# Scaling and transposing the score matrix of an attention kernel: products with a diagonal, or a scale on VectorE and transposes on TensorE

## The chip, the cores and the metric

The kernel runs on one core of a Trainium2 chip. The metric is the time of one execution on the device, in microseconds (us); lower is better. The core has five engines that run side by side and wait for each other through semaphores: TensorE for matrix products (PE in the profile, with its loading of the stationary operand shown apart as PEld), VectorE (DVE), ScalarE (ACT), GpSimd (POOL) and SyncE (SP), which here only issues transfers. Data lie in device memory, in SBUF (128 partitions) or in PSUM, into which TensorE writes.

## The reference

Two steps follow each other. The first is an attention between channels: q, k and v have the shape 4 x 6208 x 256, q and k are normalised along the 6208 rows, and a 256 x 256 matrix of scores per batch goes through a softmax.

```python
def _attn_ref(q, k, v, tau):
    qn = q / (np.linalg.norm(q, axis=1, keepdims=True) + 1e-06)
    kn = k / (np.linalg.norm(k, axis=1, keepdims=True) + 1e-06)
    s = kn.transpose(0, 2, 1) @ qn / tau
    s = s - s.max(-1, keepdims=True)
    a = np.exp(s)
    a /= a.sum(-1, keepdims=True) + 1e-09
    return (v @ a).astype(np.float32)

def _moe_ref(x, mu_k, mu_r, w_k, w_v, w_r):
    x_prev = np.concatenate([np.zeros((B, 1, D), dtype=np.float32), x[:, :-1, :]], axis=1)
    xk = mu_k * x + (1.0 - mu_k) * x_prev
    xr = mu_r * x + (1.0 - mu_r) * x_prev
    k = np.maximum(xk @ w_k, 0.0)
    v = k * k @ w_v
    r = 1.0 / (1.0 + np.exp(-(xr @ w_r)))
    return (r * v).astype(np.float32)
```

The second step takes the first one's result as x; its inner width is 1024. tau is 1.0.

## The kernel before

The rows of q and k of one batch are read in groups of up to 512 rows. For each 128 rows TensorE adds a product of q and k (two matmuls of 128 x 256, line 182) to the raw scores S in PSUM, which hold q's channels in the partitions and k's channels in the free dimension, without any norm. The sums of squares for the norms are collected beside it. The raw S is thus q's channels by k's channels, while the softmax runs over q's channels for each of k's channels. So S has to be divided by q's norms, which lie along its partitions, and turned, so that k's channels come to lie in the partitions.

The function `softmax_pieces` holds this work as pieces, to be called one at a time:

- `evac` (line 265): ScalarE copies S from PSUM to the fp32 tile `s_sb`, two halves of 128 partitions x 256.
- `roots`, `pow2`: the four columns of norms, 256 of q and 256 of k, come into the tile `rn` (128 x 4).
- `invert` (lines 257 to 260): VectorE adds a small number, takes the reciprocal, and multiplies the fp32 identity `ident_f` (128 x 128) by each of the two columns of q's reciprocal norms. The result is `rq_d`, two diagonal matrices.
- `turn` (lines 269 to 273): four fp32 products on TensorE, each with a 128 x 128 block of `s_sb` as the stationary operand and one of the diagonals as the moving one. Each writes a block of the turned and scaled S into `st_ps` in PSUM.
- `exp` (line 280): two exponentials on ScalarE from `st_ps` into `e_sb`, with k's reciprocal norms `rk` as a scale per partition, and row sums in `sm`. No maximum is subtracted, since tau bounds the scores.
- `shares`, `weigh`, `weigh_dve`: the rows are divided by their sums and give the bf16 matrix `a_sb`.

Batch 0 is summed first, in a phase of its own in which the transfers of q and k come in from SyncE's queue. At its end the pieces are called at once, with filler products between them (`keep_warm`, line 513, whose results nobody reads) and with the transposes of v's first blocks (`v_transpose_pe`, line 331). `x_first` (line 365) then makes the first block of x from `a_sb`.

After that one loop runs over 48 blocks of 512 rows of x (12 per batch) and one block of the rows left over. Each block has eight slots, j = 0 to 7. In the slots TensorE does the block's products: x from v and `a_sb` (line 352), the wide product (`up`, line 423, into `kT_ps`), the narrow products (`down`, lines 456 and 460, into `vr_ps`), and in some slots the scores of the next batch (`unit`). ScalarE takes `kT_ps` out (line 428), takes x out (line 354), squares q and k for the norms (lines 163 and 165) and makes the gate (line 469). VectorE mixes x with its previous row (line 408), squares (line 441), multiplies by the gate (line 470) and adds the squares up (line 169). When a batch's scores are complete, its pieces go into a list, in which an empty entry passes a slot; one entry is taken per slot:

```python
        return [evac, fold, None, None, norms, roots, pow2, None, invert, None, None, turn, exp, shares, None, weigh]
```

The program order on each engine is the order in which the loop writes the instructions; there is no scheduler that moves them. Plain loads with a change of type go through GpSimd's queue, v's transposing transfers and the stores through SyncE's.

Of the kernel before, what the change touches and what calls it, by code (L numbers as in the profile page):

```python
# [10 lines left out]
F32 = mybir.dt.float32  # L11
# [7 lines left out]
def kernel(  # L19
# [13 lines left out]
    nc = tc.nc  # L33
    B, N, C = q.shape
    D = C
    DF = moe_w_k.shape[1]
    P = 128
# [12 lines left out]
    pn = ctx.enter_context(tc.tile_pool(name="pn", bufs=2))  # L50
# [6 lines left out]
    ident_f = const.tile([P, P], F32, name="ident_f")  # L57
# [30 lines left out]
    st_ps = {}  # L88
# [124 lines left out]
    def softmax_pieces(b):  # L213

        s_ps, ssq_ps = cov.pop(b) if b else cov[b]
        rn = pn.tile([P, 4], F32, name="rn")
        rq_d = pn.tile([P, C], F32, name="rq_d")
        s_sb = pn.tile([P, 2, C], F32, name="s_sb")
        e_sb = pn.tile([P, 2, C], F32, name="e_sb", bufs=1)
        mx = pn.tile([P, 2], F32, name="mx")  # L220
        sm = pn.tile([P, 2], F32, name="sm")
        rk = rn[:, 2:4]
        def copies():
            cov["ssq"] = pn.tile([P, 2 * C], F32, name="ssq", tag="ssq", bufs=1)
            nc.vector.tensor_copy(cov["ssq"], ssq_ps)

        def gather():

            cov["s"] = cov[b][0]
            bank[b] = ps.tile([P, 2 * C], F32, name="bank", tag="xT_ps", bufs=2)  # L230
            for i in range(4):
                nc.tensor.matmul(bank[b][:, C + i:C + i + 1], cov["ssq"][:, i * P:(i + 1) * P], thirty2[:, 0:1],
                                 start=i == 0, stop=False, skip_group_check=True)

        def fold():
            t = pq.tile([P, 2 * C], BF16, name="sq", tag="sq", bufs=1)
            nc.vector.tensor_tensor(t, sums[b][:, 0], sums[b][:, 1], op=OP.add)
            sums[b] = t

        def norms():  # L240
            bank[b] = ps.tile([P, 2 * C], F32, name="bank", tag="xT_ps", bufs=2)
            for t, rows in ((sums.pop((b, "left"))[:, 0], L), (sums.pop(b), P)):
                for i in range(4):
                    nc.tensor.matmul(bank[b][:, C + i:C + i + 1], t[:rows, i * P:(i + 1) * P], ones[:rows, 0:1],
                                     start=rows == L and i == 0, stop=rows == P, skip_group_check=True)

        def roots():
            if b == 0:
                nc.scalar.activation(rn, bank[b][:, C:C + 4], AF.Sqrt)
            else:  # L250
                nc.scalar.copy(rn, bank[b][:, C:C + 4])

        def pow2():
            nc.gpsimd.tensor_tensor(rn, rn, half, op=OP.pow)

        def invert():
            nc.vector.tensor_scalar_add(rn, rn, 1e-6)
            nc.vector.reciprocal(rn, rn)
            for h in range(2):
                nc.vector.tensor_scalar_mul(rq_d[:, h * P:(h + 1) * P], ident_f, rn[:, h:h + 1])  # L260
            if inv_tau != 1.0:
                nc.vector.tensor_scalar_mul(rk, rk, inv_tau)

        def evac():
            nc.scalar.copy(s_sb, s_ps)

        def turn():

            st_ps[b] = ps.tile([P, 2, C], F32, name="st_ps", tag="xT_ps", bufs=2)
            for ih in range(2):  # L270
                for dh in range(2):
                    nc.tensor.matmul(st_ps[b][:, ih, dh * P:(dh + 1) * P], s_sb[:, dh, ih * P:(ih + 1) * P],  # L272
                                     rq_d[:, dh * P:(dh + 1) * P], start=True, stop=True)

        def exp():
            for ih in range(2):
                if not bounded:
                    nc.vector.tensor_reduce(mx[:, ih:ih + 1], st_ps[b][:, ih], axis=AX, op=OP.max, negate=True)
                    nc.vector.tensor_tensor(mx[:, ih:ih + 1], mx[:, ih:ih + 1], rk[:, ih:ih + 1], op=OP.mult)
                nc.scalar.activation(e_sb[:, ih], st_ps[b][:, ih], AF.Exp, scale=rk[:, ih:ih + 1],  # L280
                                     bias=0.0 if bounded else mx[:, ih:ih + 1],
                                     accum_out=sm[:, ih:ih + 1])

        def shares():
            nc.gpsimd.tensor_tensor(sm, sm, minus[:, 0:2], op=OP.pow)

        def weigh():
            for ih in range(2):
                nc.scalar.activation(a_sb[:, b, ih, :], e_sb[:, ih], AF.Copy, scale=sm[:, ih:ih + 1])

        def weigh_dve():
            for ih in range(2):
                nc.vector.reciprocal(sm[:, ih:ih + 1], sm[:, ih:ih + 1])
                nc.vector.tensor_scalar_mul(a_sb[:, b, ih, :], e_sb[:, ih], sm[:, ih:ih + 1])

        if b == 0:
            return [copies, gather, roots, evac, invert, turn, exp, weigh_dve]

        return [evac, fold, None, None, norms, roots, pow2, None, invert, None, None, turn, exp, shares, None, weigh]


# [216 lines left out]
    for g in order(0):  # L518
        group_load(0, g)
        group_cast(0, g)  # L520
        if g == DIRECT + 1:
            copies, gather, roots, evac, invert, turn, exp, weigh = softmax_pieces(0)
            copies()
            gather()
        for s in range(sizes(0)[g]):
            unit_matmul(0, g, s)
        if 5 <= g <= DIRECT:
            keep_warm(3)
        if g == NB - 1:

            nc.gpsimd.tensor_copy(gate, groups[0, g][0][:, 0, 0, 0:1])
            v_load(0)
# [25 lines left out]
    def unit(ahead=2):  # L558

        if pos["mm"] >= len(units):  # L560
            return
        u = units[pos["mm"]]
        loads_upto()
        feed(max(ahead, 1))
        unit_matmul(*u)
        pos["mm"] += 1
        feed(ahead)
        if u[1:] == (NB, S - 1):
            chain.extend(softmax_pieces(u[0]))
            holds[0] = u[0]  # L570
# [144 lines left out]
```

## Time and profile before

| | us |
|---|---|
| median of 5 runs | 515.55 |
| the five runs | 515.28, 515.55, 515.14, 518.67, 518.8 |
| the profiled execution | 515.59 |
| its span | 513.8 |
| PE busy in the span | 495.2 (96%) |
| ACT busy | 450.6 (88%) |
| DVE busy | 439.9 (86%) |
| POOL busy | 99.3 (19%) |
| PE, the four turns (line 272), 32 matmuls | 4.3 |
| DVE, the eight multiplications of line 260 | 2.1 |

The span is the time from the first to the last instruction that the profiler shows; the execution's own time is 1.8 us longer. Busy time of PE counts matmuls from start to end, and these overlap, so neighbouring matmuls can begin at less than one's duration from each other: the distance from start to start (the pitch) is what one costs in a row of them. The granted clock is the share of its full clock that TensorE was given.

### The profile page before, as it was taken

What the parts mean: (1) busy time and instruction counts of PE and PEld (TensorE: products, weight loads), DVE (VectorE), ACT (ScalarE), POOL (GpSimd) and SP (SyncE); (2) the same over time, 40 slices, a digit from 0 to 9 for tenths busy, and PEclk for the clock granted to TensorE, in tenths of its full rate; (3) what the DMA queues carried; (4) which work ended last, traced back from release to release, by engine and by line L of the source; (5) the groups of instructions that cost most, each with busy time, mean ns of one, the idle gap of its engine ahead of it and who ended that gap; (6) DMA issues with size and microseconds to landing.
All of it is one profiled execution on the core that took longest, in us unless ns stands there. A gap on an engine that the chain in (4) does not pass through costs nothing.

```text
span 513.8 us, 9496 instructions
## 1 busy us (share of the span) xinstructions
PE 495.2 (96%) x3540; PEld 336.8 (66%) x3540; DVE 439.9 (86%) x725; ACT 450.6 (88%) x924; POOL 99.3 (19%) x146
## 2 busy tenths in 40 slices
PE   4979999989999999999999999999999999999996
PEld 2455666767576767666676667667666666666675
DVE  4556899999999999999989999999878787878884
ACT  6876999999899999999899999999887888878784
POOL 0044341223045123131233223000131100000000
PEclk9989999999999999999999999999999999999999
DMA  8999999999999999998499999925497783423123
GB/s 310 409 310 189 199 152 186 150 163 197 219 176 171 204 209 167 162 171 162 89 163 184 186 184 181 192 65 124 83 168 144 109 139 84 105 76 89 42 83 103
DMA packets 133462, 83.46 MB, mean 162 GB/s; under 512 B 50660, under 2 KB 126760, under 8 KB 133416
## 3 DMA queue, kind: packets, MB, share of 16 engines
q0 software_dynamic: 56592, 33.01, 49.6%
q1 hardware_dynamic: 76656, 49.72, 42.5%
q8 instruction: 27, 0.44, 0.4%
q10 hardware_dynamic: 168, 0.13, 0.1%
q14 instruction: 19, 0.16, 0.1%
HBM read 78.71 MB, written 25.43 MB: 203 GB/s over the span
## 4 chain that ended last, share of the span: by engine, by line
PE 78%; DMA 10%; DVE 6%; ACT 4%; issue 1%; SPq 0%; DVEq 0%
PE vr_ps L460 29%; PE kT_ps L423 28%; PE vr_ps L456 7%; PE xT_ps L352 7%; PE s_ps L182 5%; DMA f<-in_k_dram 5%; DMA vT<-v_bf 5%; DVE acc L169 1%; DVE xk L408 1%; ACT kr L428 1%; DVE kk L441 1%; ACT sq L163 1%; PE st_ps L272 1%; ACT xT L354 1%; DVE delta L398 1%
## 5 line engine op out<-in xcount | busy, mean ns | idle before, releaser
L428 ACT ACTIVATE kr<-kT_ps 128x512 bf16<-128x512 f32 (+1 forms) x392 | 232.6, 605 | 28.8 <-PE kT_ps L423 24.8
L423 PE MATMUL kT_ps<-xk,w_k_sb 128*128 128x512 bf16 (+1 forms) x784 | 231.2, 377 | 0.4 <-DVE xk L408 0.2
L460 PE MATMUL vr_ps<-w_v_sb,kk 128*128 128x256 bf16 x1536 | 230.8, 273 | 0.1
L460 PEld LDWEIGHTS <-kk 128*128 128x128 bf16 x1536 | 149.7, 98 | 58.6 <-DVE kk L441 0.8
L470 DVE SCALAR_TENSOR_TENSOR res<-res,vr_ps 128x256 f32<-128x256 f32 x192 | 80.0, 417 | 45.2 <-ACT res L469 45.0
L441 DVE TENSOR_TENSOR kk<-kr 128x1536 bf16<-128x1536 bf16 (+2 forms) x148 | 117.0, 791 | 0.2 <-ACT kr L428 0.2
L423 PEld LDWEIGHTS <-w_k_sb 128*128 128x128 bf16 x784 | 75.8, 98 | 28.6 <-issue 1.2
L169 DVE TENSOR_TENSOR acc<-acc,sq 128x1024 f32<-128x1024 f32 x69 | 84.1, 1219 | 0.0
L182 PE MATMUL s_ps<-qk 128*128 128x256 bf16 x392 | 73.7, 289 | 5.0 <-DVE qk L142 5.0
L469 ACT ACTIVATE res<-vr_ps 128x256 f32<-128x256 f32 x192 | 76.2, 397 | 1.3 <-PE vr_ps L460 1.3
L456 PE MATMUL vr_ps<-w_r_sb,xr 128*128 128x256 bf16 x384 | 73.3, 272 | 1.1 <-DVE res L470 1.1
L408 DVE SCALAR_TENSOR_TENSOR xk<-delta,mu_t,xT 128x512 bf16<-128x512 bf16 x96 | 71.4, 746 | 0.0
L408 DVE SCALAR_TENSOR_TENSOR xr<-delta,mu_t,xT 128x512 bf16<-128x512 bf16 x96 | 71.4, 746 | 0.0
L456 PEld LDWEIGHTS <-xr 128*128 128x128 bf16 x384 | 37.5, 98 | 46.3 <-issue 2.4
L354 ACT CAST xT<-xT_ps 128x512 bf16<-128x512 f32 x94 | 55.4, 589 | 13.0 <-PE xT_ps L352 12.9
L352 PE MATMUL xT_ps<-vT,a_sb 128*128 128x512 bf16 x188 | 55.9, 379 | 1.6 <-DMA vT<-v_bf 1.4
L136 POOL DMA_DIRECT2D qk<-in_q_dram x39 | 26.1, 669 | 144.2 <-ACT kr L428 65.6
L165 ACT ACTIVATE sq<-qk 128x1024 f32<-128x1024 bf16 (+1 forms) x49 | 50.8, 1037 | 0.0
L182 PEld LDWEIGHTS <-qk 128*128 128x128 bf16 x392 | 39.3, 102 | 16.8 <-issue 6.8
L315 POOL DMA_DIRECT2D v_bf<-in_v_dram x48 | 37.0, 773 | 50.3 <-DMA vT<-v_bf 21.5
L398 DVE TENSOR_TENSOR delta<-xT 128x1024 bf16<-128x1024 bf16 x48 | 32.9, 686 | 1.9 <-ACT xT L354 1.8
L144 ACT ACTIVATE qk<-f 128x1024 bf16<-128x1024 f32 (+2 forms) x28 | 26.1, 948 | 8.1 <-DMA f<-in_q_dram 5.2
(82 smaller groups left out, 214.2 us busy)
## 6 DMA issues: line engine op xcount, KB each, us to landing
out_dram<-res SPq DMA_DIRECT2D x47, 512.0 KB, 4.8
v_bf<-in_v_dram POOLq DMA_DIRECT2D x48, 256.0 KB, 9.6
qk<-in_q_dram POOLq DMA_DIRECT2D x36, 256.0 KB, 8.8
qk<-in_k_dram POOLq DMA_DIRECT2D x36, 256.0 KB, 9.8
f<-in_q_dram SPq DMA_DIRECT2D x11, 512.0 KB, 9.0
f<-in_k_dram SPq DMA_DIRECT2D x11, 512.0 KB, 9.8
vT<-v_bf SPq DMA_TRANSPOSE x44, 9.4
f<-in_q_dram SPq DMA_DIRECT2D x2, 256.0 KB, 9.5
```

Of the source, the lines that this page charges most:

```text
L169: nc.vector.tensor_tensor(sums[b], sums[b], t, op=OP.add)
L182: nc.tensor.matmul(s_ps[:, ih, :], rows_at(qk, b, g, 0)[:rows, s, ih * P:(ih + 1) * P], rows_at(qk, b, g, 1)[:rows, s, :], start=t0 and ih ...
L352: nc.tensor.matmul(xT_ps, a_sb[:, b, ih, dh * P:(dh + 1) * P], vT[:, :, ih, :], start=ih == 0, stop=ih == 1)
L354: nc.scalar.copy(xT[:, dh, 1:], xT_ps)
L408: nc.vector.scalar_tensor_tensor(o[:, dh], st[i, "d"][:, dh], mu[:, dh:dh + 1], st[i, "x"][:, dh, :M], op0=OP.mult, op1=OP.add)
L423: nc.tensor.matmul(kT_ps[:, :m], w_k_sb[:, dh, fh * P:(fh + 1) * P], xk[:, dh, :m], start=dh == 0, stop=dh == 1)
L428: nc.scalar.activation(kr, kT_ps[:, :m], AF.Relu, scale=0.5 ** 0.5)
L441: nc.vector.tensor_tensor(st[i, "kk"][:, fh // 4 * 4 + lo:fh + 1, :m], kr, kr, op=OP.mult)
L456: nc.tensor.matmul(vr_ps[:, D:], xr[:, dh, s * P:(s + 1) * P], w_r_sb[:, dh, :], start=dh == 0, stop=dh == 1)
L460: nc.tensor.matmul(vr_ps[:, :D], kk[:, fh, s * P:(s + 1) * P], w_v_sb[:, fh, :], start=fh == 0, stop=fh == 7)
L469: nc.scalar.activation(res[:, s], vr_ps[:, D:], AF.Tanh, scale=0.5)
L470: nc.vector.scalar_tensor_tensor(res[:, s], res[:, s], 1.0, vr_ps[:, :D], op0=OP.add, op1=OP.mult)
```

## The change

The diagonals go. `invert` multiplies each half of `s_sb`, 128 x 256 in fp32, by the column of q's reciprocal norms that belongs to its partitions, in place. `turn` then transposes the four blocks on TensorE in its transpose mode, with `ident_f` as the moving operand.

```diff
         rn = pn.tile([P, 4], F32, name="rn")
-        rq_d = pn.tile([P, C], F32, name="rq_d")
         s_sb = pn.tile([P, 2, C], F32, name="s_sb")
...
             nc.vector.reciprocal(rn, rn)
             for h in range(2):
-                nc.vector.tensor_scalar_mul(rq_d[:, h * P:(h + 1) * P], ident_f, rn[:, h:h + 1])
+                nc.vector.tensor_scalar_mul(s_sb[:, h], s_sb[:, h], rn[:, h:h + 1])
...
             for ih in range(2):
                 for dh in range(2):
-                    nc.tensor.matmul(st_ps[b][:, ih, dh * P:(dh + 1) * P], s_sb[:, dh, ih * P:(ih + 1) * P],
-                                     rq_d[:, dh * P:(dh + 1) * P], start=True, stop=True)
+                    nc.tensor.transpose(st_ps[b][:, ih, dh * P:(dh + 1) * P], s_sb[:, dh, ih * P:(ih + 1) * P],
+                                        ident_f)
```

The number of instructions in the program and their order on each engine stay the same. In batch 0 the first multiplication now waits for ScalarE's copy of S as well as for the reciprocal, and the turn waits for VectorE alone.

## The prediction

> **What bounds the kernel now.** I read first the busy time of each engine in stretches of the span. Its columns are the stretch in us, its length, busy time and number of instructions of PE, PEld, DVE, ACT and POOL, then granted clock, DMA share and GB/s.
>
> ```profile
> 60.00:145.00 85.00, 82.46 (x594) 56.58 (x593) 82.73 (x124) 81.94 (x183) 22.27 (x35) 1.00 1.29 180
> ...
> 156.00:250.00 94.00, 94.00 (x679) 65.31 (x678) 88.52 (x140) 88.69 (x180) 22.48 (x31) 1.00 1.12 173
> ...
> 380.00:450.00 70.00, 70.00 (x485) 47.26 (x483) 57.04 (x99) 56.54 (x121) 3.55 (x5) 1.00 0.66 122
> ```
>
> From about 145 us on PE is busy for the whole of every stretch, while DVE and ACT keep some 5 us free in 94 and 13 in 70 after 380. The view of waits, cut to PE's matmuls, is empty between 145 and 510 us: there PE waits for nobody, so a PE instruction taken out should end the kernel earlier by its own length. Between 36 and 145 us it is otherwise (columns: who waited for whom, us in total, times, longest):
>
> ```profile
> PE xT_ps L352 <- DMA vT<-v_bf: 1.4, 1, 1.4
> PE vr_ps L456 <- DVE res L470: 1.1, 2, 0.7
> ```
>
> DVE is the fullest engine there (82.73 of 85 us), and a transposing DMA ends one PE wait. The chain of waits runs through that DMA from 80.88 to 106.5 us. What is won before then may be lost in that wait.
>
> **The change on PE.** The function `turn` runs once per batch. View of line 272 (ns min/median/max, first and last start), then three merged groups from the timeline (start us, length us):
>
> ```profile
> L272 PEld LDWEIGHTS st_ps<-rq_d,s_sb x32: 186/192/192, 40.3 to 372.4; 128*128 128x128 f32 x32
> L272 PE MATMUL st_ps<-rq_d,s_sb x32: 272/275/348, 40.4 to 372.5; 128*128 128x128 f32 x32
> ```
> ```profile
> 32.56 1.05 PE L232 MATMUL bank<-thirty,ssq 128*128 128x1 f32 x8 [2.16 <-DVE ssq L225]
> ```
> ```profile
> 39.24 0.61 PE L331 MATMUL vT_ps<-ident,v_bf 128*128 128x128 bf16 x8
> ```
> ```profile
> 148.50 1.05 PE L272 MATMUL st_ps<-rq_d,s_sb 128*128 128x128 f32 x8
> ```
>
> The program issues 4 products per batch, 16 in all, but the trace has 32: each fp32 product is two passes. Eight passes take 1.05 us from the first start to the last end, and one lasts 0.275, so the pitch is (1.05 - 0.275)/7 = 0.111 us, and PE gives the turn 8 x 0.111 = 0.89 us per batch. Line 232, also fp32 and also two passes each (4 products, 8 matmuls), moves one column and not 128, at the same pitch: (1.05 - 0.25)/7 = 0.114. So the fp32 weight load sets the pitch, not the number of moved columns.
>
> A transpose of fp32 is in this trace only once, in the preparation of mu (line 516), and there it is one load and one matmul:
>
> ```profile
> L516 PEld LDWEIGHTS mu_ps<-ident_f,mu_rows x1: 178/178/178, 4.0 to 4.0; 4*128 4x128 f32 x1
> L516 PE MATMUL mu_ps<-ident_f,mu_rows x1: 236/236/236, 4.0 to 4.0; 4*128 4x4 f32 x1
> ```
>
> So four transposes per batch are four passes in place of eight. Their pitch is not in the trace; its bounds are as follows. Below: the bf16 transposes of line 331, (0.61 - 0.219)/7 = 0.056 us, with a bf16 load of 98 ns. Above: load and matmul that don't overlap at all, 0.192 + 0.275 = 0.467 us. I take 0.111, since line 516's fp32 load (178 ns) is near line 272's fp32 load (192 ns) and far from the bf16 one (98 ns), and the fp32 load is what sets the pitch. Saved per batch: 0.89 - 4 x 0.111 = 0.446 us. With 0.056 it is 0.67; with 0.467 it is a loss of 0.98; at 0.223 nothing changes.
>
> In "TensorE: Matmul & The Clock Gate", section Terms, the Trainium skill says that the transpose mode of trn2 is four times faster for fp32. A quarter of a product's 0.223 would be 0.056 us per transpose, and a sum by it would end at 513.4. Line 232 speaks for less, since there the load alone holds the pitch.
>
> In batches 1, 2 and 3 the turn is followed without a gap by the next product of line 423 (149.39, 258.96, 372.62 us), inside the stretch where PE waits for nobody. I count these three whole: 3 x 0.446 = **1.34 us**.
>
> **The change on DVE.** Two multiplications of 128x128 by the diagonal's scale become two of 128x256 on S, in place.
>
> ```profile
> L260 DVE TENSOR_SCALAR rq_d<-ident_f,rn x8: 280/286/560, 39.6 to 370.6; 128x128 f32<-128x128 f32 x8
> ```
> ```profile
> L294 DVE TENSOR_SCALAR a_sb<-e_sb,sm x2: 352/352/353, 42.3 to 42.8; 128x256 bf16<-128x256 f32 x2
> ```
>
> By line 294, the same operation on 256 fp32 elements, each costs 0.352 - 0.286 = 0.07 us more, 0.14 per batch. The bound above is the rate of the fp32 additions of line 169 (1024 elements in 1.219 us, 1.19 ns each): 128 x 1.19 = 0.15 each, 0.30 per batch; below, nothing. I price it at zero in batches 1 to 3: DVE's free time hides it, and the second multiplication ended at 146.98, 256.02 and 370.89 us, while the turn's first load began at 148.28, 257.85 and 371.51: at least 0.62 us to spare against 0.30. Without this cover it would be 0.42 us in all, at most 0.9.
>
> **The new wait.** The first multiplication now waits for ACT's copy of S (line 265) as well as for the reciprocal. In batches 1 to 3 the copy is over long before (131.6 us against 146.5 in batch 1). ACT's exponential gains nothing there: it runs in its slot at 151.03, after a turn that had ended by 149.55. DVE has behind it in its queue the square of kr (line 441); it moves by at most 0.3 us and PE had no wait for it. No DMA and no queue of SP or POOL changes its order. The tile rq_d goes, which takes no time.
>
> **Batch 0** has little other work between its pieces (timeline):
>
> ```profile
> 39.65 0.63 DVE L260 TENSOR_SCALAR rq_d<-ident_f,rn 128x128 f32<-128x128 f32 x2
> ...
> 40.35 1.13 PE L272 MATMUL st_ps<-rq_d,s_sb 128*128 128x128 f32 x8
> ...
> 40.95 0.21 ACT L586 ACTIVATE gate<-ones 128x1 bf16<-128x1 bf16 x1
> ...
> 41.52 0.48 ACT L280 ACTIVATE e_sb<-st_ps,rn 128x256 f32<-128x256 f32 x1 [0.37 <-PE st_ps L272]
> ```
>
> ACT's copy of S runs from 39.06 to 39.64, the reciprocal ends at 39.62, so the new wait starts DVE at most 0.05 us later; with the 0.14 from above the transposes begin 0.19 later, at 40.54. The fourth then ends at 40.54 + 3 x 0.111 + 0.275 = 41.15, and not at 41.48. ACT is held by the loading of its table (39.65, 1.28 us) and the small activation behind it until 41.16, so the exponential can start some 0.33 us earlier than at 41.52; more than its idle 0.37 can't be won. Behind the multiplications stands DVE's copy of vT (40.20), 0.19 later; x_first, which reads it on PE, began only at 42.73. All of the 0.33 is passed on through the exponential, the weighing and x_first; yet the waits on vT's DMA and on DVE between 60 and 145 us lie ahead, and either may swallow it. Bounds 0 and 0.35; I take the middle, **0.17 us**.
>
> A rule that speaks against the change stands in the same page, "PE-mode transpose": transposes don't count as activity for the clock gate. By that rule, a window of half clock could follow the turn of batch 0. The trace has one such window, before the turn:
>
> ```profile
> 36.00:38.00 2.00, 2.00 (x32) 1.61 (x31) 0.71 (x2) 1.98 (x3) 2.00 (x4) 0.50 1.04 139
> ```
>
> The neighbouring stretches (35 to 36: clock 0.62; 38 to 39: 0.68; 1.00 on both sides) make it 0.76 + 2 + 0.64 = 3.4 us at half clock, in a phase in which PE often waits for loads. One more such window costs up to 3.4 x 0.5 = 1.7 us. The eight bf16 transposes of line 331 run at 39.24 and again at 45.14 us, and the clock stays at 1.00 from 39 to 46; four transposes of under half a us, among filler products, should not do more. Priced at zero.
>
> **Sum.** The profiled execution took 515.59 us, of which the span is 513.8; the 1.8 around it stay. 515.59 - 1.34 - 0.17 = **514.1 us**, 0.3% less. The median of the runs shown is 515.55, so nothing is added for that. Under about 0.5% (2.6 us) a measurement of this kernel can't be told from no change: three of its five runs lie within 0.4 us, two are 3 us above.
>
> **The rivals.**
>
> A, nothing arrives: a transpose has the pitch of a whole product (0.223), or PE, pulled forward, meets a wait on a transposing DMA or on kr that takes it back. For it: the trace has no full-size fp32 transpose. Against: line 516 has one pass where a product has two, and PE has no wait to be shortened after 145. Time 515.6.
>
> B, slower: in transpose mode the fp32 load no longer overlaps the matmul before it, at the four turns on PE. Pitch 0.467: 3 x 0.98 lost, and in batch 0 the fourth ends at 40.54 + 3 x 0.467 + 0.275 = 42.22, 0.74 later than before: 515.59 + 2.94 + 0.74 = 519.3. It decides from a pitch over 0.223. Against: bf16 transposes overlap (0.61 us for eight), fp32 loads do too (line 232). For: line 516 can't tell, being alone.
>
> C, one half-clock window more in batch 0: 514.1 + 1.7 = 515.8; two: 517.5. It decides from one window.
>
> D, more is won: with batch 0 earlier, the transposing DMA is issued earlier, and the waits of 1.4 and 1.1 us shown above shrink. Both gone: 514.1 - 2.5 = 511.6; it counts as faster when 1.1 of the 2.5 goes. Against: DMAs overlap there (share 1.29), so landing times need not follow issue times.
>
> **How the numbers follow.** Forecast 0.60, A 0.16, B 0.06, C 0.07, D 0.11. Faster by over 0.5% is D: 0.11. Slower by over 0.5% is B and a tail of several windows in C: 0.08. The rest, 0.81, is within. Low end of the range: pitch 0.056 and the whole of batch 0, 515.59 - 3 x 0.67 - 0.35 = 513.2, less 0.2 for the scatter of the three lower runs: 513.0. High end: no gain and one half-clock window, 515.59 + 1.7 = 517.3. B, most of D and C's tail stay outside, under 0.2.
>
> **What would show it.** Right: the trace has 16 matmuls on the transposes' line, not 32, at a pitch near 0.11 us, four in some 0.6 us; 256-element multiplications near 0.35 us; no new wait of PE after 145; and the turn of batch 2 is ahead of its old time by 0.45 us more than that of batch 1, that of batch 3 by 0.45 more again. Wrong: 32 matmuls; a pitch of 0.056 or over 0.2; PE's busy time down but its waits up by as much; granted clock under 1 beyond 39 us; a DMA wait near 106 us of another size.

## The result, and the profile after

The changed kernel takes 514.23 us (median of 54 runs) against 515.83 us of the kernel before (94 runs). The ratio is 0.9971, with a 95% interval from 0.9960 to 0.9982: about 1.5 us less, between 0.9 and 2.1.

The stretches of the span after, with the columns of the table shown before:

```profile
60.00:145.00 85.00, 81.23 (x572) 54.89 (x571) 79.83 (x120) 79.36 (x177) 19.88 (x33) 0.98 1.30 176
156.00:250.00 94.00, 94.00 (x673) 65.05 (x672) 88.95 (x141) 88.99 (x181) 24.00 (x34) 1.00 1.13 172
...
380.00:450.00 70.00, 70.00 (x486) 47.30 (x485) 57.12 (x98) 56.91 (x122) 4.07 (x6) 1.00 0.65 125
```

PE is still busy for the whole of the two later stretches. The turn and VectorE's multiplication, by the views of their lines (ns min/median/max):

```profile
L271 PEld LDWEIGHTS st_ps<-ident_f,s_sb x16: 139/141/144, 39.8 to 373.2; 128*128 128x128 f32 x16
L271 PE MATMUL st_ps<-ident_f,s_sb x16: 272/273/330, 39.8 to 373.3; 128*128 128x128 f32 x16
```
```profile
L259 DVE TENSOR_SCALAR s_sb<-s_sb,rn x8: 333/351/694, 39.0 to 372.0; 128x256 f32<-128x256 f32 x8
```

There are 16 matmuls where there were 32. One still lasts 273 ns, but in batches 1 to 3 they start 0.109 us apart (four in 0.60 us), so a turn holds PE for 4 x 0.109 = 0.44 us and not 0.89. The load in transpose mode takes 141 ns, and in the products it took 192.

This profiled execution is not a typical one: it took 516.41 us, more than 46 of the 54 runs, and 0.8 more than the profiled execution before. Its waits of PE, and the stretches around the larger one:

```profile
PE xT_ps L351 <- DMA vT<-v_bf: 2.6, 1, 2.6
...
PE vr_ps L455 <- DVE res L469: 1.1, 2, 0.7
```
```profile
103.00:107.00 4.00, 1.39 (x11) 0.88 (x9) 4.00 (x6) 2.31 (x6) 2.23 (x3) 1.00 1.34 151
107.00:111.00 4.00, 4.00 (x17) 2.07 (x16) 2.32 (x4) 2.69 (x6) 0.00 (x0) 0.57 1.18 224
```

The wait for v's transposing transfer near 106 us is 2.6 us here (1.4 before). With the clock below, these are two of the signs that the prediction named as speaking against it. The wait leaves PE with 1.39 us of work in four, and the clock in the next four falls to 0.57: the record of the clock has one period of 3.41 us at half, from 107.16. That is 1.2 us of wait more and some 1.7 us of slower products, and neither is near a turn. A second profile of the same kernel, taken later, has no such wait and no half clock near it and took 512.28 us; one of the diagonals has both (nine turns, below: a wait of 2.5 us, half clock from 108.87 us). So the two signs come with single executions and not with the change. To see the change itself, I therefore compare the starts of single instructions in two traces.

Take a product of line 423 (422 in the changed kernel), and its start in one kernel's trace less the same product's start in the other's. Around the turn of batch 1, first in the kernel before, then in the second profile of the changed kernel (start us, length us):

```profile
147.09 0.59 PE L423 MATMUL kT_ps<-xk,w_k_sb 128*128 128x512 bf16 x2
...
148.50 1.05 PE L272 MATMUL st_ps<-rq_d,s_sb 128*128 128x128 f32 x8
149.39 0.59 PE L423 MATMUL kT_ps<-xk,w_k_sb 128*128 128x512 bf16 x2
```
```profile
144.96 0.59 PE L422 MATMUL kT_ps<-xk,w_k_sb 128*128 128x512 bf16 x2
...
146.37 0.60 PE L271 MATMUL st_ps<-ident_f,s_sb 128*128 128x128 f32 x4
146.81 0.59 PE L422 MATMUL kT_ps<-xk,w_k_sb 128*128 128x512 bf16 x2
```

Ahead of the turn the difference is -2.13 us, behind it -2.58. The table has this difference in us, in each field for the last such product ahead of a turn and for the first one behind it.

| start in, less start in | batch 1 | batch 2 | batch 3 |
|---|---|---|---|
| changed (profile above), before | 2.022, 1.568 | 1.652, 1.198 | 1.278, 0.824 |
| changed (second profile), before | -2.125, -2.579 | -2.487, -2.941 | -2.832, -3.286 |

Each turn brings 0.454 us, in both profiles, whatever had happened ahead of it. Between the turns a little is given back: in the second profile 0.09 us behind batch 1's and 0.11 behind batch 2's (-2.941 to -2.832), in the first 0.08 and 0.08. From ahead of the first of these turns to behind the last, the changed kernel wins 1.20 us in the first profile and 1.16 in the second.

### The profile page after: what moved, and what is told of

Read it like the earlier page. It is cut to its first block, busy times and chain, and to the rows that moved or that the text cites. A ratio compares the mean times of both kernels' runs of the same rounds, so it can differ in the third digit from the quotient of the medians.

```text
span 514.6 us, 9464 instructions
## 1 busy us (share of the span) xinstructions
PE 493.8 (96%) x3524; PEld 334.3 (65%) x3524; DVE 441.0 (86%) x725; ACT 450.1 (87%) x924; POOL 99.9 (19%) x146
## 5 line engine op out<-in xcount | busy, mean ns | idle before, releaser
L182 PE MATMUL s_ps<-qk 128*128 128x256 bf16 x392 | 72.6, 286 | 5.8 <-DVE qk L142 5.7
```

The lines of the kernel that those rows point to most:

```text
L182: nc.tensor.matmul(s_ps[:, ih, :], rows_at(qk, b, g, 0)[:rows, s, ih * P:(ih + 1) * P], rows_at(qk, b, g, 1)[:rows, s, :], start=t0 and ih ...
```

## Experiments

In the expectations the theory is the prediction's: PE's time in batches 1 to 3 is passed on whole, and batch 0 counts for little. Ratios are to the kernel before, on the same chip, with their 95% intervals.

### Which part brings the gain

**Products with the identity.** VectorE scales S as in the change, TensorE works as before.

```diff
-                    nc.tensor.transpose(st_ps[b][:, ih, dh * P:(dh + 1) * P], s_sb[:, dh, ih * P:(ih + 1) * P],
-                                        ident_f)
+                    nc.tensor.matmul(st_ps[b][:, ih, dh * P:(dh + 1) * P], s_sb[:, dh, ih * P:(ih + 1) * P],
+                                     ident_f, start=True, stop=True)
```

> VectorE scales S as in the changed kernel, but TensorE turns it by ordinary fp32 products with the identity, so the eight passes per batch come back. Theory (the gain is the fp32 passes taken off PE): 32 matmuls again at 0.111 us, ratio to the kernel before 1.000, about 1.5 us slower than the changed kernel. Rival (the gain comes from the work on VectorE, the tile rq_d that went, or the other order of waits): ratio 0.997, as in the changed kernel.

Measured: 0.9992 (0.9970 to 1.0014). The time alone hardly excludes the rival's 0.997. The trace does: against the kernel before, a product ahead of and behind the turn stands at -1.926 and -1.926, -1.931 and -1.931, -1.932 and -1.932 us in the three batches. From ahead of batch 1's turn to behind batch 3's the two traces keep step to 0.006 us, with the larger multiplications on VectorE in one of them. VectorE's part costs nothing there and brings nothing; the gain of these three batches is in the passes.

**Batches apart.** Each kernel takes the new code in the batches named and the old in the others.

```diff
-                nc.vector.tensor_scalar_mul(rq_d[:, h * P:(h + 1) * P], ident_f, rn[:, h:h + 1])
+                if b > 0:
+                    nc.vector.tensor_scalar_mul(s_sb[:, h], s_sb[:, h], rn[:, h:h + 1])
+                else:
+                    nc.vector.tensor_scalar_mul(rq_d[:, h * P:(h + 1) * P], ident_f, rn[:, h:h + 1])
```

The turn is split by the same condition; the other kernel has `b == 0` in its place.

> The change in batches 1 to 3 only; batch 0 keeps its diagonals. Theory: these three turns stand where PE waits for nobody, 3 x (8 x 0.1115 - 4 x 0.109) = 1.37 us, ratio 0.9973. Rival (the gain comes from batch 0, ahead of the loop): ratio 1.000.

> The change in batch 0 only. Theory: the exponential of batch 0 follows S's copy in the same time as before (2.46 us after its start), and what would be won is lost in the wait for the transposing transfer near 106 us: ratio 1.000, within 0.1%. Rival (batch 0 brings the gain): ratio 0.997. My prediction had 0.17 us for this part: 0.9997, which is too near to the theory to be told apart by the time; the profile has to tell it.

Measured: 0.9983 (0.9973 to 0.9993) for batches 1 to 3, so 0.9 us less (0.4 to 1.4); 0.9993 (0.9979 to 1.0006) for batch 0, so 0.4 us less, and no change at all is not excluded. The later batches bring a gain without batch 0, as the theory said; its 0.9973 lies at the edge. Batch 0's time can't be told from none, and its profile decides against my expectation of 2.46 us from S's copy to the exponential:

```profile
38.70 0.58 ACT L268 COPY s_sb<-s_ps 128x512 f32<-128x512 f32 x1
...
39.33 0.71 DVE L261 TENSOR_SCALAR s_sb<-s_sb,rn 128x256 f32<-128x256 f32 x2
...
39.84 0.80 PE L276 MATMUL st_ps<-ident_f,s_sb 128*128 128x128 f32 x4
...
40.59 0.21 ACT L593 ACTIVATE gate<-ones 128x1 bf16<-128x1 bf16 x1
40.70 0.46 ACT L287 ACTIVATE e_sb<-st_ps,rn 128x256 f32<-128x256 f32 x1
```

Here it is 2.00 us, and the exponential starts without idle time behind ACT's small activation, which follows the loading of its table. In the first profile of the changed kernel it was 2.46 (the timeline's columns are start and length):

```profile
38.18 0.58 ACT L264 COPY s_sb<-s_ps 128x512 f32<-128x512 f32 x1
...
38.70 0.92 POOL L580 DMA_DIRECT2D w_v_sb<-in_moe_w_v_dram  x1
...
39.04 0.95 DVE L259 TENSOR_SCALAR s_sb<-s_sb,rn 128x256 f32<-128x256 f32 x2
39.57 0.80 POOL L314 DMA_DIRECT2D v_bf<-in_v_dram  x1
...
39.79 0.80 PE L271 MATMUL st_ps<-ident_f,s_sb 128*128 128x128 f32 x4 [1.04 <-DVE s_sb L259]
...
40.63 0.48 ACT L279 ACTIVATE e_sb<-st_ps,rn 128x256 f32<-128x256 f32 x1 [0.36 <-PE st_ps L271]
```

The pair of multiplications takes 0.95 us in place of 0.71, since the first one lasted 694 ns here and 454 in the other. PE waits for it, and ACT for PE. Nine profiles have transposes in batch 0: in six of them the distance is 2.00 us (first multiplication 355 to 555 ns), in three 2.46 (692 to 694 ns). With the diagonals it is 2.27 us in the profiles of the kernel with batches 1 to 3 changed and of the nine turns below (409 and 408 ns), and 2.47 in that of the kernel before (560 ns). So batch 0 wins 0.27 to 0.47 us where ACT's table sets the start of the exponential; where the first multiplication is held up longest, it wins nothing or loses up to 0.19. How often each case occurs is not known.

### What a pass costs, and whether PE's time is passed on

**Nine turns in place of one** in batches 1 to 3, over the same result; once with the transposes, once with the products of the kernel before.

```diff
-            for ih in range(2):
+            for ih in [0, 1] * (9 if b > 0 else 1):
```

> The changed kernel with each turn of batches 1 to 3 done nine times over, with the same result: 8 x 4 x 3 = 96 transposes more. Theory (PE's time there is passed on whole, at a pitch of 0.109 us): 10.5 us more than the changed kernel, 524.7 us, ratio to before 1.017. Rival (other engines set the pace and hide part of it): less than 5 us more, ratio under 1.007.

> The kernel before with each turn of batches 1 to 3 done nine times over, with the same result: 8 x 8 x 3 = 192 fp32 passes more. Theory: at 0.1115 us each and passed on whole, 21.4 us more than the kernel before, 537.2 us, ratio 1.0415, so twice what the transposes cost. Rival (part of it hidden): well under 1.04.

Measured: 1.0190 (1.0171 to 1.0208) with transposes, 1.0443 (1.0414 to 1.0472) with products. The starts behind the turns, as in the table above:

| start in, less start in | batch 1 | batch 2 | batch 3 |
|---|---|---|---|
| nine transposed, changed (second profile) | 1.829, 5.322 | 5.224, 8.717 | 8.603, 12.096 |
| nine with diagonals, before | 3.009, 10.156 | 10.147, 17.294 | 17.282, 24.429 |

A batch grows by 3.493 us, which is 32 x 0.1092, and by 7.147 us, which is 64 x 0.1117. Between the batches 0.10 and 0.11 us of the first are won back and 0.01 of the second. So a pass is 0.11 us in either mode, and PE's time there comes out all but whole at the end. Neither rival stands. (The time of the first, 1.0190, lies a little above the 1.017 expected; it has four runs only, and the steps in the trace are as expected.)

The first of the two also bears on the rule on the clock gate that the prediction weighed:

```profile
148.20 4.09 PE L271 MATMUL st_ps<-ident_f,s_sb 128*128 128x128 f32 x36
```
```profile
148.80:152.00 3.20, 3.20 (x32) 3.20 (x30) 3.20 (x6) 0.73 (x2) 0.00 (x0) 1.00 0.58 80
152.20:156.00 3.80, 3.80 (x29) 2.65 (x28) 0.08 (x1) 3.24 (x10) 1.14 (x2) 1.00 0.80 207
```

For 3.2 us PE has nothing but transposes, and the granted clock (last but two) is 1.00 then and in the 3.8 us behind. All half-clock periods of this trace, at 32.7 and 520.8 us, lie at whole multiples of 3.413 us from each other; on this grid one period runs from 148.78 to 152.19, and the 36 transposes fill it but for its last 0.06 us. The turns of batches 2 and 3 (from 260.80 and 377.50 us) fill such a period all but 0.10 and 0.03 us, and the clock is 1.00 in and behind them too. The Trainium skill, "TensorE: Matmul & The Clock Gate", section "PE-mode transpose", says that the full clock does not engage for transpose mode, since it does not count as busy in the same way; fp32 transposes in a row, begun at full clock, kept it in this trace.

**What sets the pitch.** 16 fp32 transposes more behind the turn: of 64 stationary columns in batch 1, of 64 rows in batch 2, whole ones in batch 3.

```diff
+            for n in range(16):
+                ih, dh = n // 2 % 2, n % 2
+                if b == 1:
+                    nc.tensor.transpose(st_ps[b][:64, ih, dh * P:(dh + 1) * P], s_sb[:, dh, ih * P:ih * P + 64],
+                                        ident_f)
+                if b == 2:
+                    nc.tensor.transpose(st_ps[b][:, ih, dh * P:dh * P + 64], s_sb[:64, dh, ih * P:(ih + 1) * P],
+                                        ident_f[:64, :64])
+                if b == 3:
+                    nc.tensor.transpose(st_ps[b][:, ih, dh * P:(dh + 1) * P], s_sb[:, dh, ih * P:(ih + 1) * P],
+                                        ident_f)
```

> The changed kernel with 16 fp32 transposes more behind the turn: in batch 1 with half of the columns in the stationary operand (128x64), in batch 2 with half of the rows (64x128, so 64 moved columns), in batch 3 whole ones. Theory (the fp32 load, by its columns, sets the pitch, as line 232 showed for products): 0.055 us in batch 1, 0.109 in batches 2 and 3. Rival (the moved fp32 columns set it): 0.109 in batches 1 and 3, 0.055 in batch 2. If both take as long: 0.109 everywhere.

Measured, in the timeline (start, length of the group of 16):

```profile
146.68 1.75 PEld L276 LDWEIGHTS st_ps<-ident_f,s_sb 128*64 128x64 f32 x16
146.78 1.91 PE L276 MATMUL st_ps<-ident_f,s_sb 128*64 128x128 f32 x16
```
```profile
257.73 1.08 PEld L279 LDWEIGHTS st_ps<-ident_f,s_sb 64*128 64x128 f32 x16 [0.17 <-issue]
257.74 1.22 PE L279 MATMUL st_ps<-ident_f,s_sb 64*128 64x64 f32 x16
```
```profile
372.10 1.91 PE L282 MATMUL st_ps<-ident_f,s_sb 128*128 128x128 f32 x16
```

Half the stationary columns shorten the load (111 ns in place of 141) and leave the pitch at (1.91 - 0.27)/15 = 0.109 us. Half the moved columns bring it to 0.062 (the starts behind the first two). My theory of the load falls for transposes, and the rival's side holds: the pitch goes with the moved operand. The second kind has half the rows as well as half the moved columns, and no run varied the rows alone. In the bf16 products of line 182 half the rows don't shorten the pitch (0.119 us with 64 rows, 0.109 with 128), so the columns are the likelier cause.

**bf16 transposes.** VectorE writes the scaled S as bf16, and `turn` takes the bf16 identity; S is rounded ahead of the exponential.

```diff
-                nc.vector.tensor_scalar_mul(s_sb[:, h], s_sb[:, h], rn[:, h:h + 1])
+                nc.vector.tensor_scalar_mul(s_bf[:, h], s_sb[:, h], rn[:, h:h + 1])
...
-                    nc.tensor.transpose(st_ps[b][:, ih, dh * P:(dh + 1) * P], s_sb[:, dh, ih * P:(ih + 1) * P],
-                                        ident_f)
+                    nc.tensor.transpose(st_ps[b][:, ih, dh * P:(dh + 1) * P], s_bf[:, dh, ih * P:(ih + 1) * P],
+                                        ident)
```

> The changed kernel with the scaled S written as bf16 and turned by bf16 transposes (S is rounded to bf16 ahead of the exponential). By the bf16 transposes of v, pitch 0.056 us against 0.109: 12 x 0.053 = 0.64 us less than the changed kernel, ratio to before 0.996. If the four transposes are held by something other than the load of an fp32 operand: 0.997.

> The bf16 transposes again (S rounded to bf16), beside the changed kernel on the same chip: 12 x 0.053 = 0.64 us less than it, so 0.0012 less in the ratio.

Measured: 0.9976 (0.9961 to 0.9992), and 0.9966 (0.9951 to 0.9980) beside the changed kernel's 0.9974. In the trace the pitch is 0.056 us, and each turn brings 0.214 us more (starts in the second run's trace less those in the second profile of the changed kernel: 1.940 to 1.726, 1.938 to 1.724, 1.930 to 1.716); 0.21 and 0.21 of it are given back behind the turns of batches 1 and 2. So of the 0.64 us expected some 0.22 are left at the end of this trace. The times can't show whether it beats the changed kernel.

### The early phase, and VectorE's cover

**Three turns in batch 0** of the kernel before: the loop of the nine turns, with 3 and `b == 0`.

> The kernel before with the turn of batch 0 alone done three times over: 16 fp32 passes more, 1.78 us on PE ahead of the loop. Theory (the transposing transfer that PE waits for near 106 us lands at a time of its own, so time won or lost before it is swallowed): the wait there shrinks by about 1.4 us, and the time rises by 0.4 us at most, ratio 1.000 to 1.001. Rival (batch 0's time is passed on whole): 1.78 us more, ratio 1.0035.

Measured: 1.0043 (1.0026 to 1.0060), 2.2 us more (1.3 to 3.1). My theory fell and the rival stands: time lost in batch 0 reaches the end. Its profile shows no wait on a transposing transfer at all. Among the 14 profiles of this study, four have one that ends between 105 and 108 us (1.4 to 2.6 us: the kernel before, the changed one, nine turns with diagonals, the second bf16 one), and that of batch 0 alone has two shorter ones (0.7 us near 105, 0.9 near 116). It comes and goes: of the changed kernel's two profiles one has it. That time won ahead of it is lost where it comes is likely, but not shown.

**Transfers ahead of the store.**

```diff
-            if j == 5 and 4 <= i + 5 < NBLK - 1:
+            if j == 1 and 4 <= i + 5 < NBLK - 1:
```

> The changed kernel with the transposing transfers of v issued in slot 1 of a block in place of slot 5, so that in SyncE's queue they stand ahead of a store and do not wait behind it. If the wait near 106 us (2.6 us in the profile of the changed kernel) is due to the late issue: it goes, and with it 1.5 to 3 us; ratio to before 0.992 to 0.994. If the transfers' own rate sets the landing: as the changed kernel, 0.997, with the wait still there.

Measured: 0.9975 (0.9958 to 0.9991), as the changed kernel. The profile has no wait near 106 us, but one of 1.24 us at 122, for the transfer of v's last rows. Since the wait is missing in most profiles anyway, this doesn't tell what brings it; that stays open.

**More scaling.** Four more multiplications per batch in batches 1 to 3, into a tile that is not read.

```diff
+            for h in [0, 1] * (2 if b > 0 else 0):
+                nc.vector.tensor_scalar_mul(s_x[:, h], s_sb[:, h], rn[:, h:h + 1])
             for h in range(2):
                 nc.vector.tensor_scalar_mul(s_sb[:, h], s_sb[:, h], rn[:, h:h + 1])
```

> The changed kernel with four more multiplications of 128x256 per batch in batches 1 to 3, into a tile that nobody reads: 12 x 0.27 us = 3.2 us more on VectorE, six times what the change adds there. Theory (VectorE's free time hides it, as the prediction priced it): the time of the changed kernel, ratio to before 0.997. Rival (VectorE sets the pace there): up to 3.2 us more, ratio 1.003.

> The changed kernel itself, for the runs beside it: ratio 0.997. In its profile, batch 0's exponential follows the start of S's copy in 2.0 us (as in the profiles with the change in batch 0 that were taken since), not in 2.46 as in the first profile of the changed kernel.

Measured: 1.0017 (1.0002 to 1.0033) against the changed kernel's 0.9974 (0.9955 to 0.9993): the rival, for this amount. PE's waits between 145 and 380 us, where the changed kernel's second profile has none, are below; the first belongs to batch 1, the other to batch 2, and in batch 3 it is the load of the turn that begins late.

```profile
PE vr_ps L458 <- DVE res L472: 0.8, 1, 0.8
PE vr_ps L462 <- DVE kk L443: 0.3, 1, 0.3
```

Of some 1.08 us added per batch, 1.05, 0.45 and 0.46 reach PE, by the starts. VectorE's free time around this slot is under a microsecond; the 0.14 us of the change fit into it, and what the run adds, over six times as much, doesn't. The expectation of 2.0 us in batch 0 of the changed kernel's second profile was a miss: it is 2.46 again, with a first multiplication of 692 ns.

## Why the prediction was right

The forecast of 514.1 us met 514.23. The path was right; the size of its main term came out right by luck, since the reason given for it was not.

- **PE sets the pace after 145 us**: shown. Nine turns cost 3.493 and 7.147 us per batch more than one, all but 0.1 us passed on.
- **0.446 us per batch**: measured 0.454. The size was right, its reason wrong: I held the fp32 load for what sets the pitch, since line 232 has the same pitch with one moved column. For products that row still speaks for it, though no run varied their load. In transpose mode half the columns of the load leave the pitch at 0.109 and half the moved block brings it to 0.062, so there it is not the load. That 0.109 is so near to the 0.111 that I took was luck.
- **The factor of four** that the Trainium skill gives ("TensorE: Matmul & The Clock Gate", Terms) is not what the trace shows: a product's two passes take 0.223 us and a transpose 0.109, a factor of 2.05. The sum by four, 513.4 of 515.59, is a ratio of 0.9958, just outside the measured interval (from 0.9960); the pitch settles it.
- **1.34 us for the three batches**: 3 x 0.454 = 1.36 on PE, of which 0.16 to 0.20 come back between the turns (behind batch 1's ahead of a product of line 459, whose operand VectorE writes), so 1.16 to 1.20. From turn to turn the lead grows by 0.35 to 0.37 us and not by the 0.45 that was to show it right. The prediction had no such term; it is its rival A in small, PE pulled forward into a wait.
- **VectorE at zero**: right for 0.14 us (two traces keep step to 0.006 us). My reading that some 5 us free in 94 are a broad cover was too generous: in this slot 1.08 us more are not covered. (The copy of S in batch 1, which I put at 131.6 us, starts then and ends at 132.27, still long before.)
- **Batch 0 at 0.17, between 0 and 0.35**: in the profiles it is from -0.19 to 0.47, and in most 0.27 or more. The limit by ACT's table load was real: it sets the 2.00 us. I priced the multiplication at 0.07 us more than before; in batch 0 the first one lasted 355 to 694 ns, and where it is longest it takes the gain. Whether the transfer's wait takes any of it, as I had it, is not shown. The time of batch 0 alone (0.4 us less, or none) can't decide.
- **Sum**: 1.16 to 1.20 and between -0.19 and 0.47 make 1.0 to 1.7, against 1.5 measured (0.9 to 2.1). The interval is wide; the account rests on the steps in the traces.
- **Rivals**: A falls with the turns' steps, but for the 0.16 to 0.20 above, and B with the pitch. C falls with the clock: it is 1.00 from 42 to 103 us in all nine profiles with transposes in batch 0. The one half-clock period inside the loop in the first profile after follows a wait for a transfer. D didn't come: the wait on DVE stays at 1.1 and 1.2 us in the two profiles after, and the one on the transfer comes and goes.

## What to carry to other kernels

Where the profile shows an engine that waits for nobody, take the pitch of the instruction in a row, not its duration, times the number removed. That is what can be won there at most; here 1.36 us on PE left 1.16 to 1.20. Comparing the starts of the same instruction on both sides of the edit in two traces shows it to some hundredths of a microsecond when the times scatter by three. Count passes: one fp32 product was two here. A single profiled execution may be slower than the one before while the kernel is faster: look for the one long wait before explaining it.

## What the hardware showed beside

In 12 of the 14 profiles VectorE's first multiplication of batch 0 began 0.28 to 0.63 us into the issue of a transfer by GpSimd. Whenever it began, it ended 0.12 us behind that issue's end (0.05 for the 128x128 ones of the diagonals), and so it lasted from 403 to 694 ns. In the two others it began after an issue had ended, and it took 355 ns (128x256) and 289 ns (128x128), as in the later batches. But the second multiplication of 128x256, begun some 0.1 us into the next issue, took its usual 333 ns, and the reciprocals within an issue took 178, so the rule is not plain, and keeping GpSimd quiet there was not tried.

The load in transpose mode is shorter than in an fp32 product (141 against 192 ns), and its length falls with its columns (111 ns for 64).
